# First chunk in halves of 256 tokens with six feature tiles ahead, two token tiles transposed by DMA, parameter arithmetic on GpSimd

## The chip, the cores and the metric

The kernel runs on one core of a Trainium2 chip. The metric is the device time of one execution in microseconds. Before the change it is 179.42 us, the median of 3 runs (179.28 to 179.64). The engines are named as in the profile: PE (TensorE matmul; PEld is its weight load), DVE (VectorE), ACT (ScalarE), POOL (GpSimd) and SP (SyncE, here only an issuer of DMAs). Each engine works off its own instructions in program order.

## What is computed

The input x is 2048 tokens of 512 features in bfloat16. It is normalised (layer norm without weights) to xn, and two layers of xn are added to x:

```python
xn = layernorm(x)
# A: a diagonal complex recurrence with 512 states
Lam_bar = exp(exp(log_dt) * (Lambda_re + 1j * Lambda_im))
B_bar   = ((Lam_bar - 1) / Lambda)[:, None] * (B_re + 1j * B_im)
Bu      = xn @ B_bar.T
h[t]    = Lam_bar * h[t - 1] + Bu[t]
A       = 2 * (h @ C.T).real + xn * Dskip
# B: a gated feed-forward layer with 1376 hidden features
Bf      = (silu(xn @ w_gate) * (xn @ w_up)) @ w_down
out     = x + A + Bf
```

## The kernel before, in words

**Tiling.** The 2048 tokens are four chunks of 512 (`NCH` = 4, `CW` = 512), each of four token tiles of 128 (`TPC` = 4). The hidden features are eleven feature tiles (`FT` = 11): ten of 128, and a last one of 96 whose columns are packed in their own tiles (`w_last`, `wu_last`). Every contraction over the 512 input features takes four matmuls (`KD` = 4) with the weights as the stationary operand and `xnT`, the normalised tokens transposed to features by tokens, as the moving one.

**Stages of one chunk.** `bproj_chunk` projects the chunk on the eight blocks of B (real and imaginary part, four blocks of states each; L357), ACT copies the results to SBUF (L359). `gateup_tile` makes gate and up of one feature tile (eight matmuls of 512 columns, L432), ACT evicts them from PSUM (Silu on L446, a cast on L447), DVE multiplies them in pairs (L451, queued in `products`). `ssm_ops` is the recurrence on DVE: a rotation by tables of cosine and sine (L367 to L381), eight scans (L399), a rotation back. `out_chunk` makes the output tiles on PE: `out_ffn` (L528) and `out_ssm` (L545).

**Order of the work.** The order of PE is written out. The work of DVE and part of ACT's lies in a `backlog`, a list of pieces with a cost each; `pump(us)` releases pieces as PE's work, in us, is written, `need(tag)` releases all that carry a tag, `multiply(keep)` releases products. For chunk 0 PE's order is: feature tiles 0 to 2 in pieces as the tokens come (`head_mm`, L631), tiles 3 to 6, the eight B projections, tiles 7 to 9, the last tile; then chunk 1 with `bproj_chunk(1)`.

**The head.** Nine dummy matmuls of 512 columns (L608) come first. For each of the four token tiles of chunk 0, DVE makes statistics (L185, L186), ACT makes 1/sqrt(var + eps) as Exp(-0.5 * Ln(var + eps)) (L190, L191), DVE normalises (L203), PE transposes in four blocks (L220), and ACT or DVE copies the two halves to `xnT` (L227, L229). The gate and up results of tiles 0 to 2 are kept in six of the eight PSUM banks until all 512 tokens are in. The 12 rows of parameters are transposed on PE as well (L250), cast by DVE (L253), and lead through `params_a`, `params_a2` and `params_sin` to the step `ws2` of the tables and the start values; between them ACT loads another function table (L259).

**Chunk 1's tokens.** `ln_rest(1, False)` gives its statistics (on DVE), a power on POOL (L195), four norms (L203, on DVE) and, after each, a DMA transpose on SP's queue (`xT_dma`, L234). They stand in the backlog with `table_ops`: for two of the four state blocks at a time a piece `turns` (L271), two pieces `half` (L277, L279, L280) on DVE, two sines on ACT (L284).

**Loads.** SP's queue issues x, the weights in the groups of `fgroups` (`load_w1`, L112), B transposed (L142), later the rest (`load_late`); ACT's queue issues three of the first ones; POOL's queue the parameters. DMAs from SP and ACT share eight semaphores in turn, so that each waits for the one eight places before it.

Of the kernel before, what the change touches and what calls it, by code (L numbers as in the profile page):

```python
# [23 lines left out]
def kernel(  # L24
# [17 lines left out]
    nc = tc.nc  # L42
# [30 lines left out]
    def bank(shape=(128, CW), dtype=F32):  # L73
        return psum.tile(list(shape), dtype, name="ps")
# [39 lines left out]

    neg_half = const.tile([128, TPC], F32, name="neg_half")
    nc.vector.memset(neg_half[:], -0.5)
    eps_t = const.tile([128, 1], F32, name="eps_t")
    nc.vector.memset(eps_t[:], EPS)

    nc.scalar.preload_act_table_set("natural_log_exp_and_others")  # L120

# [14 lines left out]
    for n in (TPC, TPC + 2):  # L136
        nc.sync.dma_start(out=xall[:, n:n + 2, :], in_=x_v[:, n:n + 2, :])
    load_w1(nc.sync, wg_g, wg_v, 2)
    load_w1(nc.sync, wu_g, wu_v, 2)
    for part, src in enumerate((A_B_re, A_B_im)):  # L140
        for k in range(KD):
            nc.sync.dma_start_transpose(out=BT[:, part, k, :], in_=src[:, k * 128:(k + 1) * 128])  # L142
        if part == 0:
            load_w1(nc.sync, wg_g, wg_v, 3)
            load_w1(nc.sync, wu_g, wu_v, 3)

    nc.sync.dma_start(out=w_last[:, :, 0:LB + LA], in_=wg_v[:, :, FL:F])
    nc.sync.dma_start(out=w_last[:, :, LB + LA:128], in_=wu_v[:, :, FL + LB:F])

    def load_late():  # L150
        nc.sync.dma_start(out=wu_last[:], in_=wu_v[:, :, FL:FL + LB])
# [29 lines left out]
    def xn_tile(c):  # L181
        return xn_end if c == NCH - 1 else xall[:, c * TPC:(c + 1) * TPC, :]
# [4 lines left out]

    def rstd_act(n):

        nc.scalar.activation(out=ve[:, n:n + 1], in_=mv[:, n, 1:2], func=ACT.Ln, bias=eps_t[:, 0:1])  # L190
# [10 lines left out]
    def norm_dve(n):  # L201
        c, i = divmod(n, TPC)
        nc.vector.tensor_scalar(out=xn_tile(c)[:, i, :], in0=xall[:, n, :], scalar1=mv[:, n, 0:1],  # L203
                                scalar2=rstd[:, n:n + 1], op0=ALU.subtract, op1=ALU.mult)

    def norm_act(n):
# [3 lines left out]

    HK = KD // 2

    def xT_pe(n, on_dve=(), prm_too=False):

        c, i = divmod(n, TPC)
        for h in range(2):
            tp = bank((128, HK * 128 + 128), BF16)
            for k in range(HK):
                lo = (h * HK + k) * 128
                nc.tensor.transpose(out=tp[:, k * 128:(k + 1) * 128], in_=xn_tile(c)[:, i, lo:lo + 128],  # L220
                                    identity=ident[:])
            if prm_too and h == 1:
                prm_transpose(tp[:, HK * 128:])
            dst = xnT[:, h * HK:(h + 1) * HK, n * 128:(n + 1) * 128]
            src = tp[:, 0:HK * 128].rearrange("p (k t) -> p k t", k=HK)
            if h in on_dve:
                nc.vector.tensor_copy(out=dst, in_=src)  # L227
            else:
                nc.scalar.copy(out=dst, in_=src)  # L229
        return tp[:, HK * 128:]  # L230

    def xT_dma(n):
        c, i = divmod(n, TPC)
# [12 lines left out]
    kk, fs1, fc1 = sm("kk", 2, NQ), sm("fs1", 2, NQ), sm("fc1", 2, NQ)  # L246
    V = nc.vector

    def prm_transpose(pp):
        nc.tensor.transpose(out=pp, in_=prm_rows[:], identity=ident[:])  # L250
# [44 lines left out]
    def tt(o, a, b, op):  # L295
        V.tensor_tensor(out=o, in0=a, in1=b, op=op)

    def params_sin():

        def turns(dst, shift):  # L300
            src = ws2[:]
            if shift:
                V.tensor_scalar(out=dst[:], in0=src, scalar1=shift, scalar2=None, op0=ALU.add)
                src = dst[:]
            V.tensor_scalar(out=kk[:], in0=src, scalar1=MAGIC, scalar2=MAGIC, op0=ALU.add, op1=ALU.subtract)
            tt(dst[:], src, kk[:], ALU.subtract)

        V.tensor_scalar(out=ws2[:, 1, :], in0=ws2[:, 0, :], scalar1=float(CW), scalar2=None, op0=ALU.mult)
        turns(fs1, 0.0)
        nc.scalar.activation(out=sin1[:], in_=fs1[:], func=ACT.Sin, scale=TWO_PI_LO)  # L310
        turns(fc1, 0.25)
        nc.scalar.activation(out=cos1[:], in_=fc1[:], func=ACT.Sin, scale=TWO_PI_LO)

    def params_b():
        tt(t_a[:], lre, lre, ALU.mult)
        tt(t_b[:], lim, lim, ALU.mult)
        tt(den[:], t_a[:], t_b[:], ALU.add)
        V.reciprocal(out=den[:], in_=den[:])
        tt(lbi[:], r_t[:], sin1[:, 0, :], ALU.mult)
        tt(lbr[:], r_t[:], cos1[:, 0, :], ALU.mult)  # L320
        V.tensor_scalar(out=lbr[:], in0=lbr[:], scalar1=-1.0, scalar2=None, op0=ALU.add)
        tt(t_a[:], lbr[:], lre, ALU.mult)
        tt(t_b[:], lbi[:], lim, ALU.mult)
        tt(num_re[:], t_a[:], t_b[:], ALU.add)
        tt(t_a[:], lbi[:], lre, ALU.mult)
        tt(t_b[:], lbr[:], lim, ALU.mult)
        tt(num_im[:], t_a[:], t_b[:], ALU.subtract)
        for dst, num, s in ((c2re, num_re, 2.0), (nc2re, num_re, -2.0), (nc2im, num_im, -2.0)):
            V.scalar_tensor_tensor(out=dst[:], in0=num[:], scalar=s, in1=den[:], op0=ALU.mult, op1=ALU.mult)

    def c_ops():

# [266 lines left out]

    GU = 8 * 0.2163  # L600
    BP = 4 * 0.2163
    H = 3
    held = [(bank(), bank()) for _ in range(H)]
    warm = held[0][0]

    def dummy(n, cols):
        for _ in range(n):
            nc.tensor.matmul(warm[:, 0:cols], lhsT=ones[:, 0:128], rhs=ones[:, 0:cols], start=True, stop=True)  # L608
# [15 lines left out]

    def head_mm(which, lo, hi, ks, fis):

        for fi in fis:
            for k in ks:  # L630
                nc.tensor.matmul(held[fi][which][:, lo * 128:hi * 128], lhsT=wslice((wg_g, wu_g)[which], fi, k),  # L631
                                 rhs=xnT[:, k, lo * 128:hi * 128], start=(k == 0), stop=(k == KD - 1))

    allk = range(KD)
# [12 lines left out]
    head_mm(0, 0, 1, range(0, HK), (0, 1))  # L647
    head_mm(0, 0, 1, range(HK, KD), (0, 1))
    xT_pe(1)
    rstd_act(2)  # L650
    head_mm(1, 0, 1, range(0, HK), (0, 1))
    head_mm(1, 0, 1, range(HK, KD), (0, 1))
# [4 lines left out]
    head_mm(0, 1, 2, range(0, HK), (0, 1))  # L657
    head_mm(1, 1, 2, range(0, HK), (0, 1))
    head_mm(0, 1, 2, range(HK, KD), (0, 1))
    head_mm(1, 1, 2, range(HK, KD), (0, 1))  # L660
    head_mm(0, 0, 2, allk, (2,))
    pp = xT_pe(2, on_dve=(0, 1), prm_too=True)
    head_mm(1, 0, 2, allk, (2,))
    norm_dve(3)
    params_a(pp)
    params_a2()
    head_mm(0, 2, 3, range(0, HK), range(H))
    head_mm(1, 2, 3, range(0, HK), range(H))
    xT_pe(3, on_dve=(0, 1))
    head_mm(0, 2, 3, range(HK, KD), range(H))  # L670
    head_mm(1, 2, 3, range(HK, KD), range(H))
# [7 lines left out]
    for fi in range(H):  # L679
        head_mm(0, 3, 4, allk, (fi,))  # L680
        head_mm(1, 3, 4, allk, (fi,))
        gu_out(0, fi, *held[fi])
        pump(GU / 4)
    pump(2.0)

    def bproj_chunk(c):
        need(f"ln{c}")
# [130 lines left out]
```

## Time and profile before

| what | value |
|---|---|
| median of 3 runs | 179.42 us |
| span of the profiled execution, first to last instruction | 177.3 us (its own time is not listed apart from the runs; the median lies 2.1 above the span) |
| mean granted PE clock by the record | 1.00 |
| PE transposes in the head | 16 of features, 1 of parameters |
| DMA transpose of a token tile: issue, to landing | 1.22 us, 2.4 us |
| Silu eviction and cast of 128x512 on ACT | 0.62 and 0.60 us |
| `params_b` on DVE, 16 operations on 128x4 | 31.99 to 34.02 us |

A row of a timeline gives the start from the beginning of the span, the length, the engine, the line of the kernel, the operation, what it writes and reads, the shape and how many instructions the row merges; in square brackets stands idle time before it and what ended that. The names are the program's: `ps` is a PSUM bank, `xall` the tokens, `pm` a scratch tile. "SPq" rows are the times in which SP's queue issues DMAs, not those in which data moves.

### The profile page before, as it was taken

The page shows a single profiled execution, that of the slowest core. Times are in us where ns is not written, and L with a number is a line of the kernel's source. Part 1 is how long each engine was busy: PE and PEld are TensorE (multiplying, and loading weights), DVE is VectorE, ACT ScalarE, POOL GpSimd, SP SyncE. Part 2 cuts the span into 40 slices and gives each one's busy share as a digit, 9 for nine tenths or more (in the row PEclk, how much of TensorE's full clock was granted, in tenths as well). Part 3 has the DMA queues.
Part 4 walks back from the last instruction along what each step waited for, and adds up shares of the span by engine and source line. Part 5 has one row for each costly group of instructions (what it writes and reads, how often), then busy time and mean ns, then how long its engine had stood idle before and what let it go on. Part 6 is the DMA issues. An engine that isn't in the chain of part 4 may idle for free.

```text
span 177.3 us, 2449 instructions
## 1 busy us (share of the span) xinstructions
PE 172.9 (97%) x900; PEld 83.6 (47%) x916; DVE 154.4 (87%) x238; ACT 94.7 (53%) x173; POOL 23.2 (13%) x29
## 2 busy tenths in 40 slices
PE   8999999999999999999999999999999999999993
PEld 2884444444444444444444444444444444444743
DVE  6789997999999977899999999999999999990033
ACT  4589696977499369914966662013766600220000
POOL 6003000001200140000700000014280000150000
DMA  5999749973041024900440000005469500072012
GB/s 163 316 264 239 148 90 261 334 126 89 0 96 26 0 52 96 355 0 0 60 62 2 0 0 4 0 0 61 58 97 177 86 0 0 0 85 33 4 50 69
DMA packets 29131, 15.53 MB, mean 88 GB/s; under 512 B 18848, under 2 KB 29056, under 8 KB 29088
## 3 DMA queue, kind: packets, MB, share of 16 engines
q1 hardware_dynamic: 24416, 11.41, 28.8%
q0 software_dynamic: 3456, 3.28, 13.7%
q10 hardware_dynamic: 1248, 0.69, 1.3%
q8 instruction: 7, 0.11, 0.3%
q14 instruction: 4, 0.03, 0.1%
HBM read 8.03 MB, written 5.24 MB: 75 GB/s over the span
## 4 chain that ended last, share of the span: by engine, by line
PE 98%; issue 1%; DVE 0%
PE ps L432 36%; PE ps L528 19%; PE ps L545 16%; PE ps L357 16%; PE ps L631 3%; PE ps L608 2%; PE ps L483 2%; PE ps L535 2%; PE ps L472 1%; PE ps L220 1%; DVE res L548 0%; PE ps L250 0%
## 5 line engine op out<-in xcount | busy, mean ns | idle before, releaser
L432 PE MATMUL ps<-xnT,wg 128*128 128x512 bf16 x144 | 37.8, 379 | 0.4
L432 PE MATMUL ps<-xnT,wu 128*128 128x512 bf16 x145 | 37.3, 379 | 0.0
L528 PE MATMUL ps<-wd_sb,guT 128*128 128x512 bf16 (+2 forms) x177 | 36.7, 355 | 0.2
L399 DVE TENSOR_TENSOR_SCAN g<-r_t,car,u 128x512 bf16<-128x512 f32 x24 | 28.8, 1264 | 0.0
L545 PE MATMUL ps<-CF,wt 128*128 128x512 bf16 (+2 forms) x141 | 28.2, 355 | 0.2
L357 PE MATMUL ps<-xnT,BT 128*128 128x512 bf16 x126 | 28.2, 379 | 0.1
L446 ACT ACTIVATE guT<-ps 128x512 bf16<-128x512 f32 x40 | 24.6, 615 | 5.0 <-PE ps L432 5.0
L447 ACT CAST u<-ps 128x512 bf16<-128x512 f32 x40 | 24.1, 602 | 5.2 <-PE ps L432 5.1
L528 PEld LDWEIGHTS <-guT 128*128 128x128 bf16 x180 | 16.9, 98 | 18.0
L432 PEld LDWEIGHTS <-wu 128*128 128x128 bf16 x148 | 14.5, 98 | 17.5
L432 PEld LDWEIGHTS <-wg 128*128 128x128 bf16 x148 | 14.4, 98 | 17.2
L555 ACT CAST res<-ps 128x512 bf16<-128x512 f32 x12 | 6.7, 594 | 28.1 <-PE ps L545 28.1
L556 POOL DMA_DIRECT2D out_dram<-res x12 | 10.5, 1041 | 78.0 <-ACT res L555 78.0
L545 PEld LDWEIGHTS <-wt 128*128 128x128 bf16 x144 | 13.4, 98 | 14.4 <-issue 0.4
L357 PEld LDWEIGHTS <-BT 128*128 128x128 bf16 x128 | 12.5, 98 | 15.1
L359 ACT CAST u<-ps 128x512 bf16<-128x512 f32 x32 | 17.6, 588 | 3.7 <-PE ps L357 3.6
L451 DVE TENSOR_TENSOR guT<-guT,u 128x1024 bf16<-128x1024 bf16 x20 | 13.5, 680 | 0.0
L548 DVE TENSOR_TENSOR res<-ps,xn_end 128x512 bf16<-128x512 f32 (+2 forms) x6 | 3.0, 514 | 11.8 <-PE ps L545 11.8
L195 POOL TENSOR_TENSOR rstd<-ve,neg_half 128x4 f32<-128x4 f32 x3 | 5.3, 1761 | 53.9 <-DVE ve L194 53.9
L367 DVE TENSOR_TENSOR pm<-u,c 128x2048 bf16<-128x2048 bf16 x8 | 9.8, 1221 | 1.2 <-ACT c L284 1.1
L185 DVE BATCH_NORM_STATS2 stats<-xall 128x6 f32<-128x512 bf16 x14 | 9.5, 676 | 0.4 <-DMA xall<-in_A_x_dram 0.4
L367 DVE TENSOR_TENSOR pm<-g,c 128x2048 bf16<-128x2048 bf16 x8 | 9.7, 1215 | 0.1
(108 smaller groups left out, 166.6 us busy)
## 6 DMA issues: line engine op xcount, KB each, us to landing
out_dram<-in_A_x_dram SPq DMA_DIRECT2D x1, 1536.0 KB, 7.0
out_dram<-res POOLq DMA_DIRECT2D x12, 128.0 KB, 3.0
out_dram<-xall POOLq DMA_DIRECT2D x3, 512.0 KB, 7.6
wd_sb<-in_B_w_down_dram SPq DMA_DIRECT2D x1, 1280.0 KB, 10.9
xall<-in_A_x_dram SPq DMA_DIRECT2D x1, 1024.0 KB, 6.1
xall<-in_A_x_dram SPq DMA_DIRECT2D x2, 256.0 KB, 4.6
wg<-in_B_w_gate_dram SPq DMA_DIRECT2D x1, 512.0 KB, 5.6
wu<-in_B_w_up_dram SPq DMA_DIRECT2D x1, 512.0 KB, 6.1
```

Source lines behind the costliest of these rows:

```text
L185: nc.vector.bn_stats(out=stats[:, n, :], in_=xall[:, n, :])
L357: nc.tensor.matmul(ps[:], lhsT=BT[:, part, k, q * 128:(q + 1) * 128], rhs=xnT[:, k, c * CW:(c + 1) * CW], start=(k == 0), stop=(k == KD - 1))
L359: nc.scalar.copy(out=u_tiles[c][:, part, q, :], in_=ps[:])
L367: V.tensor_tensor(out=t[:], in0=flat(src()[:, i]), in1=flat(tab[:]), op=ALU.mult)
L399: V.tensor_tensor_scan(out=g()[:, part, q, :], data0=r_t[:, q:q + 1].to_broadcast([128, CW]), data1=u_tiles[c][:, part, q, :], initial=ini ...
L432: nc.tensor.matmul(ps[:fs, lo:hi], lhsT=wslice(groups, fi, k), rhs=xnT[:, k, c * CW + lo:c * CW + hi], start=(k == 0), stop=(k == KD - 1))
L446: nc.scalar.activation(out=guT[:fs, fi, :], in_=psg[:fs], func=ACT.Silu)
L447: nc.scalar.copy(out=u_pair[c][:fs, fi % 2, :], in_=psu[:fs])
L451: products.append(lambda: V.tensor_tensor(out=g, in0=g, in1=u, op=ALU.mult))
L528: nc.tensor.matmul(o[:], lhsT=gu_tiles[c][:, fi, i * 128:(i + 1) * 128], rhs=wd_sb[:, fi, lo:hi], start=(fi == 0), stop=False)
L545: nc.tensor.matmul(o[:], lhsT=w_tiles[c][:, part, q, i * 128:(i + 1) * 128], rhs=CF[:, part, q, lo:hi], start=False, stop=(c > 0 and part ...
L556: nc.gpsimd.dma_start(out=out_v[:, n, :], in_=res[:], accum_op=ALU.add)
```

## The change

It has these parts:

- The weight groups are tiles 0-1, 2-3, 4-5 and 6-9. ACT's queue issues up of group 1 and both of group 2; SP's queue issues group 3, the tokens of chunk 1 (as one DMA) and B's transposes after the DMA transposes of token tiles 2 and 3 (`load_mid`). POOL's queue issues `w_last`, from the backlog behind chunk 1's statistics.
- Token tile 0 and 1 are normalised in two halves of 256 features; each half is transposed on PE and copied (first half DVE, second half ACT). Token tiles 2 and 3 are transposed by DMA.
- PE makes feature tiles 0 to 5 for the first 256 tokens, then for the second 256. A PSUM bank holds 256 tokens of two feature tiles; ACT evicts and DVE multiplies 512 columns at a time. Tiles 6 to 9 follow in full, and the eight B projections come after them (`G0` = 10), then the last tile.
- The sine tables stand further ahead in the backlog: five pieces ahead of chunk 1's statistics, two between these and the norms, three after.
- `params_b` runs on POOL but for its reciprocal; it multiplies by `den` in two operations of its own.
- `eps` is an immediate, not a tile.

The order of instructions that the changed program gives each engine: on ACT, Ln and Exp of token tile 1 stand behind the copy of token tile 0's second half; on DVE, the cast of the parameters stands behind the norm of token tile 3, and ahead of chunk 1's norms stand two `turns` pieces, three `half` pieces, six products of 512 columns, two of 1024 and the statistics. PE's first matmul of chunk 1's projection waits for the four DMA transposes of chunk 1.

```diff
-    fgroups = [(0, 2), (2, 3), (3, 7), (7, FT - 1)]
+    fgroups = [(0, 2), (2, 4), (4, 6), (6, FT - 1)]
...
-    load_w1(nc.sync, wu_g, wu_v, 1)
+    load_w1(nc.scalar, wu_g, wu_v, 1)
+    load_w1(nc.scalar, wg_g, wg_v, 2)
...
+    def load_mid():
+        load_w1(nc.sync, wg_g, wg_v, 3)
+        load_w1(nc.sync, wu_g, wu_v, 3)
+        nc.sync.dma_start(out=xall[:, TPC:2 * TPC, :], in_=x_v[:, TPC:2 * TPC, :])
+        for part, src in enumerate((A_B_re, A_B_im)):
+            for k in range(KD):
+                nc.sync.dma_start_transpose(out=BT[:, part, k, :], in_=src[:, k * 128:(k + 1) * 128])
+
+    def load_w_last():
+        nc.gpsimd.dma_start(out=w_last[:, :, 0:LB + LA], in_=wg_v[:, :, FL:F])
+        nc.gpsimd.dma_start(out=w_last[:, :, LB + LA:128], in_=wu_v[:, :, FL + LB:F])
...
-    def xT_pe(n, on_dve=(), prm_too=False):
+    def xT_pe(n, h, on_dve):
...
     def params_b():
-        tt(t_a[:], lre, lre, ALU.mult)
+        gt(t_a[:], lre, lre, ALU.mult)
...
         V.reciprocal(out=den[:], in_=den[:])
-        tt(lbi[:], r_t[:], sin1[:, 0, :], ALU.mult)
+        gt(lbi[:], r_t[:], sin1[:, 0, :], ALU.mult)
...
+        gt(num_re[:], num_re[:], den[:], ALU.mult)
+        gt(num_im[:], num_im[:], den[:], ALU.mult)
...
     dummy(9, CW)
     ln_stats(0)
     rstd_act(0)
+    load_w1(nc.scalar, wu_g, wu_v, 2)
     nc.vector.bn_stats(out=stats[:, 1, :], in_=xall[:, 1, :])
-    norm_dve(0)
+    norm_dve(0, 0, DH)
+    xT_pe(0, 0, True)
+    norm_dve(0, DH, D)
+    dummy(1, 128)
+    xT_pe(0, 1, False)
+    dummy(2, 128)
     nc.vector.bn_aggr(out=mv[:, 1, :], in_=stats[:, 1, :])
     rstd_act(1)
-    xT_pe(0, on_dve=(0,))
-    dummy(4, 128)
-    norm_dve(1)
+    head_mm(held, (0, 1), 0, 0, 1, kh[0])
+    head_mm(held, (0, 1), 0, 0, 1, kh[1])
+    norm_dve(1, 0, DH)
+    norm_dve(1, DH, D)
+    xT_pe(1, 0, True)
+    xT_pe(1, 1, False)
+    head_mm(held, (0, 1), 1, 0, 1)
     ln_stats(2)
     rstd_act(2)
     nc.vector.bn_stats(out=stats[:, 3, :], in_=xall[:, 3, :])
     norm_dve(2)
+    xT_dma(2)
     nc.vector.bn_aggr(out=mv[:, 3, :], in_=stats[:, 3, :])
     rstd_act(3)
     norm_dve(3)
+    xT_dma(3)
+    load_mid()
+    head_mm(held, (0, 1), 0, 1, 2, kh[0])
+    head_mm(held, (0, 1), 0, 1, 2, kh[1])
+    head_mm(held, (0, 1), 1, 1, 2)
+    pp = prm_transpose()
+    head_mm(held, (2, 3), 0, 0, 2)
     params_a(pp)
     params_a2()
     params_sin()
+    head_mm(held, (2, 3), 1, 0, 2)
+    head_mm(held, (4, 5), 0, 0, 2)
+    head_mm(held, (4, 5), 1, 0, 2)
     tables = table_ops()
     stats1, norm1 = ln_rest(1, False)
-    queue("ln1", stats1)
-    queue("tables", tables[:2])
+    queue("tables", tables[:5])
+    queue("ln1", stats1 + [(0.0, load_w_last)])
+    queue("tables", tables[5:7])
     queue("ln1", norm1)
-    queue("tables", tables[2:])
+    queue("tables", tables[7:])
...
+    more()
+    head_out(held, 0, 0)
+    head_mm(second, pairs[0], 0, 2, 3)
+    head_mm(second, pairs[0], 1, 2, 3)
+    pump(GU / 2)
...
-    G0 = 7
-    for fi in range(H, G0):
+    G0 = FT - 1
+    for fi in range(2 * NP, G0):
```

More of the change, by code (lines that the diff above doesn't have):

```diff
@@ L211 @@
     HK = KD // 2
-    def xT_pe(n, on_dve=(), prm_too=False):
+    def xT_pe(n, h, on_dve):
         c, i = divmod(n, TPC)
[L216 to L230, printed above, removed]
+        tp = bank((128, HK * 128), BF16)
+        for k in range(HK):
+            lo = (h * HK + k) * 128
+            nc.tensor.transpose(out=tp[:, k * 128:(k + 1) * 128], in_=xn_tile(c)[:, i, lo:lo + 128], identity=ident[:])
+        dst = xnT[:, h * HK:(h + 1) * HK, n * 128:(n + 1) * 128]
+        src = tp[:].rearrange("p (k t) -> p k t", k=HK)
+        if on_dve:
+            nc.vector.tensor_copy(out=dst, in_=src)
+        else:
+            nc.scalar.copy(out=dst, in_=src)
     def xT_dma(n):
@@ L247, with prm_transpose @@
     V = nc.vector
-    def prm_transpose(pp):
-        nc.tensor.transpose(out=pp, in_=prm_rows[:], identity=ident[:])
+    def prm_transpose():
+        pp = bank((128, 128), BF16)
+        nc.tensor.transpose(out=pp[:], in_=prm_rows[:], identity=ident[:])
+        return pp
     def params_a(pp):
@@ L623, in ln_rest, with head_mm, head_out @@
         return ops, tail
-    def head_mm(which, lo, hi, ks, fis):
+    def head_mm(sets, fis, which, lo, hi, ks=range(KD)):
+        base = lo * 128 // HALF * HALF
         for fi in fis:
+            p, j = place[fi]
             for k in ks:
-                nc.tensor.matmul(held[fi][which][:, lo * 128:hi * 128], lhsT=wslice((wg_g, wu_g)[which], fi, k),
+                nc.tensor.matmul(sets[p][which][:, j, lo * 128 - base:hi * 128 - base],
+                                 lhsT=wslice((wg_g, wu_g)[which], fi, k),
                                  rhs=xnT[:, k, lo * 128:hi * 128], start=(k == 0), stop=(k == KD - 1))
-    allk = range(KD)
+    def head_out(sets, p, half):
+        if half == 0:
+            head_u[p] = up_p.tile([128, 2, CW], BF16, name="u2")
+        cols = slice(half * HALF, (half + 1) * HALF)
+        a, b = pairs[p]
+        g, u = gu_tile(0)[:, a:b + 1:b - a, cols], head_u[p][:, :, cols]
+        nc.scalar.activation(out=g, in_=sets[p][0][:], func=ACT.Silu)
+        nc.scalar.copy(out=u, in_=sets[p][1][:])
+        products.append(lambda: V.tensor_tensor(out=g, in0=g, in1=u, op=ALU.mult))
+    pairs = ((0, 2), (1, 3), (4, 5))
+    place = {fi: (p, j) for p, fis in enumerate(pairs) for j, fi in enumerate(fis)}
+    head_u = {}
+    kh = (range(0, HK), range(HK, KD))
+    DH = D // 2
     dummy(9, CW)
@@ new lines @@
+    head_mm(second, pairs[0], 1, 2, 3)
+    pump(GU / 2)
+    more()
+    head_out(held, 1, 0)
+    head_mm(second, pairs[1], 0, 2, 3)
+    head_mm(second, pairs[1], 1, 2, 3)
+    pump(GU / 2)
+    multiply(1)
+    head_out(held, 2, 0)
+    for p in range(2):
+        head_mm(second, pairs[p], 0, 3, 4)
+        head_mm(second, pairs[p], 1, 3, 4)
+        head_out(second, p, 1)
+        pump(GU / 2)
+        multiply(1)
+    more()
+    head_mm(second, pairs[2], 0, 2, 4)
+    head_mm(second, pairs[2], 1, 2, 4)
@@ L686, in bproj_chunk @@
+    head_out(second, 2, 1)
+    pump(GU)
+    multiply(1)
     def bproj_chunk(c):
```

78 lines of the change are left out of this document (24 added, 54 removed).

## The prediction

> **What bounds the kernel now.** I read the page's busy times and the chain that ended last, then PE's timeline of the first 40 us, then the timelines of DVE and of SP's queue around the first chunk border. First the page:
>
> ```profile
> PE 172.9 (97%) x900; PEld 83.6 (47%) x916; DVE 154.4 (87%) x238; ACT 94.7 (53%) x173; POOL 23.2 (13%) x29
> ...
> PE 98%; issue 1%; DVE 0%
> ```
>
> PE works from 0.78 us to the end and the last chain is PE itself. So the time is PE's own work plus any wait the change puts before a matmul; work taken from or given to DVE, ACT or POOL counts only through such a wait. PE's timeline (start, length, instruction):
>
> ```profile
> 0.78 4.00 PE L608 MATMUL ps<-const-bfloat16-1.0 128*128 128x512 bf16 x9 [0.78 <-PEq L802]
> 4.76 0.61 PE L220 MATMUL ps<-ident,xall 128*128 128x128 bf16 x4
> ...
> 9.50 0.39 PE L220 MATMUL ps<-ident,xall 128*128 128x128 bf16 x4
> 9.72 0.50 PE L631 MATMUL ps<-xnT,wg 128*128 128x128 bf16 x6
> ...
> 11.73 1.03 PE L432 MATMUL ps<-xnT,wg 128*128 128x512 bf16 x3
> ...
> 31.59 7.07 PE L357 MATMUL ps<-xnT,BT 128*128 128x512 bf16 x31
> ```
>
> Two things to see. Four transposes cost PE 0.22 us (9.50 to 9.72), 56 ns each. And at 31.59 PE starts chunk 1's B projection, the first work that needs the tokens of chunk 1. DVE and SP's queue make those tokens:
>
> ```profile
> 13.60 0.66 DVE L185 BATCH_NORM_STATS2 stats<-xall 128x6 f32<-128x512 bf16 x1
> ...
> 14.59 0.88 DVE L271 TENSOR_SCALAR pm<-jidx,ws 128x512 f32<-128x512 f32 x2
> 15.50 0.69 DVE L279 TENSOR_SCALAR pm<-pm 128x1024 f32<-128x1024 f32 x1
> 16.23 1.22 DVE L280 SCALAR_TENSOR_TENSOR pm<-pm 128x1024 f32<-128x1024 f32 x1
> 17.37 0.69 DVE L451 TENSOR_TENSOR guT<-guT,u 128x1024 bf16<-128x1024 bf16 x1
> 17.97 1.38 DVE L203 TENSOR_SCALAR xall<-xall,mv,rstd 128x512 bf16<-128x512 bf16 x4
> ```
>
> ```profile
> 20.06 5.16 SPq L234 DMA_TRANSPOSE xnT<-xall  x4
> ```
>
> The four norms run at 17.97, the four DMA transposes issue from 20.06, 1.31 us apart, and land 2.4 to 2.5 us after issue: the last at 26.5, 5.1 us before PE needs it. That margin is what I check the change against.
>
> **The change, part by part** (times in us from the span's start; durations by the rows of before).
>
> *PE's work.* Eight transposes and one 128-column dummy go: 9 x 0.056 = -0.50. The matmul columns of feature tiles 0 to 5 in chunk 0 are equal (96 x 128 + 48 x 256 against 80 x 128 + 8 x 256 + 24 x 512), and 256 columns take 0.109, so smaller pieces cost nothing.
>
> *Token tile 0, in halves.* The first rstd is there at 4.29 in both. A half norm is not in the trace; between the 512-wide norm (0.41) and the 256-wide copy (0.29) I take 0.29. Then: norm half 4.29 to 4.58, transposes 4.64 to 5.03, DVE copy 5.07 to 5.36. The second half norm stands behind that copy on DVE: 5.28 to 5.57, transposes to 5.89, ACT copy 5.93 to 6.30. In before that copy started at 5.41: the second half is 0.5 later, the first 0.1 earlier.
>
> *Token tile 1.* Its Ln and Exp now stand behind that ACT copy; in before they stood ahead. Copy at 5.93, Ln at 6.20, Exp 6.52 to 6.73 (0.33 and 0.20 by their rows), half norms from 6.76 (before: 5.40), transposes 7.10 to 7.57, copies to 7.98. PE waits about 0.3 and then 0.5 here. Tiles 0 and 1 through feature tiles 0 and 1 are finished at 8.75; in before at 7.68. **+1.07**.
>
> *Feature tiles 2 to 5 for the first half:* 32 x 0.109, PE at 12.29 with the parameter transpose. Their weights are 1 MB behind the first 1 MB; in before 2.25 MB had landed at 10.3 (wg of 512 KB issued at 4.70, landing 5.6 later), so the last, wanted at 11.4, should be there by 10.5. Cost nothing; if that cover were gone, a few tenths.
>
> *Token tiles 2 and 3 by DMA.* DVE's copy, statistics and norms put tile 2's norm at 9.13 to 9.54 and tile 3's, behind ACT's Ln and Exp, at 10.23 to 10.64. Transposes issue at 9.58 and 10.88 and land 2.5 later: 12.1 and 13.4. PE wants them at 12.29 and 14.1. Hidden by 0.2 and 0.7.
>
> *PSUM.* The parameter cast now stands behind tile 3's norm on DVE: 10.55 (before 9.15). Through dt, dre and r_t (0.86), the table load (1.28) and two sines, ACT's first eviction comes at 12.9 (before 11.51), one each 0.48. Pair 1's second-half banks are pair 0's first-half ones: PE waits for them from 13.18 to 13.55 and a little at 14.0. **+0.39**. Six feature tiles are done at 18.0, before 16.92: +1.07 - 0.44 (transposes) + 0.39 and roundings, **+1.1**. All four remaining feature tiles (6.92) and chunk 0's B projection (6.92) and the last feature tile (0.87) follow, and PE is at chunk 1's projection at 32.7.
>
> *SP's queue* passes the moved loads: weights of tiles 6 to 9 at 12.2 and 12.8, x at 13.4, eight BT transposes 14.0 to 24.4. By 1.5 us per 512 KB these land at 15.4, 16.9, 18.4, BT's halves by 20.5 and 26; wanted at 18.0, 18.9, 21.1, 24.9 and 28.4. Hidden.
>
> *Chunk 1's norms, the term that decides.* In the new order DVE does before them: two turns, two "half" pieces of the sine tables, six products of 512, the statistics, two products of 1024, the other two turns and a third half. By start-to-start rows: turns 0.91 and 0.79; halves 1.87, 2.60, 1.85; statistics with ve 3.40; products 6 x 0.33 (half of 0.60 plus a little) and 2 x 0.60: 14.6 us of work, from 12.24 (end of the parameter chain), so 26.9 at the least. It also waits: 0.85 for the first evicted pair (ACT, 13.97), 0.65 for the fifth product (evicted 17.8), 0.25 for tile 9 (26.15). First norm at **28.6** (before 17.97). Then 0.41, four issues 1.31 apart, and 2.5 to land: 28.6 + 0.41 + 3 x 1.31 + 2.5 = 35.5, where PE stands since 32.7. **A wait of 2.8**, behind which all of PE's order stands.
>
> *GpSimd.* DVE loses 15 of 16 small operations (2.03 by 31.99 to 34.02), off the path. POOL gets 17. No such POOL row exists: bounds 0.10 (memset of one column) and 1.97 (the slowest pow on 128x4). I take 0.3, next to the 128x128 select (0.29), as pow is a long function. They have from 28 to 46.5, where POOL's next pow is due: nothing. The last feature tile's weights, now POOL's DMAs (0.5 to 1.04 each, landing within 4.6), land by 32.7 at the latest, wanted at 31.8; a delay would fall inside the 2.8.
>
> *After 35.5.* PE has the same 145.7 us left. DVE is about 3.0 behind its old place when chunk 0's rotation is done (the cosine table is late behind ACT's evictions), PE 3.9, so DVE is not worse off. SP's later transposes: C's issue ends at about 51.6 (before 42.9), chunk 2's tokens land near 59, wanted at 60.7. Nothing, with 1.5 to spare.
>
> **Sum:** 35.5 against 31.59, **+3.9**. The PE losses ahead of 32.7 are absorbed in it. The profiled span is 177.3; the runs' median 179.42 lies 2.1 above it, which I keep: 177.3 + 3.9 + 2.1 = **183.3**.
>
> **Clock.** The dummies of 512 columns stand 0.43 apart, later matmuls 0.216: PE is at half rate until about 5.35, though the clock column says 1.00. The new order leaves PE idle a few tenths before that point and 2.8 us at 32.7. *TensorE: Matmul & The Clock Gate* of the Trainium skill (What's actually happening) has the clock halved after an idle window of some 3.4 us and released after a busy one. By that rule 2.8 us is just not enough; if it were, a window at half rate would lose about 1.7 (an estimate from that page), 185.0. No row of before shows PE idle this long.
>
> **Rivals.**
> 1. *Chunk 1 is in time and only the head loses.* PE at 32.7: 177.3 + 1.1 + 2.1 = 180.5. It needs the norms at 25.8. Against: 14.6 us of DVE work after 12.24. For: I may have ACT's evictions and DVE's products too slow. 0.10.
> 2. *Faster: PE only loses work.* Half norms bring tile 1 no later and chunk 1 is ready: -0.5, 178.9. It decides if chunk 1's first norm starts by 24.2 (31.1 - 2.5 - 3.9 - 0.4). For: the eight transposes do go, and the tiles arrive by DMA in time. Against: Ln and Exp behind the ACT copy, and the same 14.6. 0.05.
> 3. *The idle PE falls back to half rate.* At the start half rate lasted 4.6 us, so up to 2.3 lost: 185.6. Decides if the wait grows past what the clock tolerates, which before can't show. 0.08.
> 4. *POOL's small operations are slow.* Over 1.1 us each, 17 of them pass 46.5, delay chunk 2's rstd and with it DVE, which waits in order for it: at 1.66, some 10 late, 187 and more. For: pow's 1.47 to 1.97 on the same shape. 0.05.
>
> **How the numbers follow.** Forecast 0.72, within 182.0 to 184.7 (a microsecond of DVE or ACT either way). The range takes in half of rival 3 and leaves out rivals 1, 2 and 4, 0.20: **181.2 to 185.4**. A measurement tells about 0.2% from no change. Faster 0.05; same 0.02 (between rivals 1 and 2); slower 0.93.
>
> **What would show it.** Chunk 1's first norm near 28.6 on DVE; SP's four transposes of xnT from 29 on; a PE gap of about 3 us before chunk 1's projection, released by the last of them; tile 1's norm near 6.8; a first eviction near 12.9. Wrong: norms before 26, no gap on PE, or a gap elsewhere (weights of tiles 2 to 5, PSUM, chunk 2's tokens).

## The result, and the profile after

The changed kernel takes 185.47 us in the median of four runs (183.23, 184.84, 186.10, 186.19), the kernel before beside it on the same chip 179.35 us (179.18 to 179.64). It is **slower**: the ratio is 1.026 (95% interval 1.023 to 1.029). This ratio is taken from the two faster runs of the changed kernel, 184.04 us on average, because the other two lie more than 1.5% above its fastest. Forecast were 183.3 us, 181.2 to 185.4: the two faster runs lie inside that range, 186.10 and 186.19 above it.

Three of the four runs show a mean PE clock of 0.99, and only the fastest shows 1.00. The profiled execution (span 184.4 us) is the slowest of the four. Its page:

```profile
PE 177.0 (96%) x939; PEld 87.3 (47%) x939; DVE 153.3 (83%) x224; ACT 97.1 (53%) x172; POOL 35.5 (19%) x48
...
PEclk9999999969999999999999999999999999999999
...
PE 93%; ACT 3%; DVE 1%; DMA 1%; issue 0%
```

PE is busy for 4.1 us more although 0.5 us of its work was taken away; one slice of the clock row, the ninth (36.9 to 41.5 us), reads 6 where all others read 9; and the last chain is no longer PE alone. PE's timeline (start, length, instruction, idle before it):

```profile
5.89 0.39 PE L217 MATMUL ps<-ident,xall 128*128 128x128 bf16 x2 [0.53 <-DVE xall L201]
...
8.77 1.06 PE L636 MATMUL ps<-xnT,wg 128*128 128x128 bf16 x8
9.62 0.76 PE L636 MATMUL ps<-xnT,wu 128*128 128x128 bf16 x8
...
13.76 0.61 PE L636 MATMUL ps<-xnT,wg 128*128 128x128 bf16 x8
...
32.90 1.03 PE L485 MATMUL ps<-xnT,w_last 128*128 128x512 bf16 x4
36.94 8.75 PE L359 MATMUL ps<-xnT,BT 128*128 128x512 bf16 x32 [3.02 <-ACT c L279]
```

Three things are to be seen. Eight matmuls of 128 columns take 1.06 us at 8.77 and 0.61 at 13.76: PE is at half rate until about 9.85 us, where in the kernel before it was until 5.35. Then PE stands idle for 3.02 us before chunk 1's B projection. And the 32 matmuls of that projection take 8.75 us, in the kernel before 7.07. What PE waits for, on DVE and SP's queue:

```profile
29.86 1.40 DVE L201 TENSOR_SCALAR xall<-xall,mv,rstd 128x512 bf16<-128x512 bf16 x4
```

```profile
30.32 5.16 SPq L227 DMA_TRANSPOSE xnT<-xall  x4
```

Chunk 1's norms begin at 29.86 (before: 17.97) and the transposes issue from 30.32. By the trace's DMA records they land at 32.74, 34.07, 35.37 and 36.70; PE starts at 36.94. The row names ACT's cosine table as releaser, because that instruction ended at 36.79, after the last landing. Which of the two counts is the first question to the chip.

The stretch around the resumption (start:end and length, busy time and instruction count of PE, PEld, DVE, ACT and POOL, the granted clock, DMA share, GB/s):

```profile
34.00:37.00 3.00, 0.06 (x1) 0.09 (x2) 0.18 (x1) 2.75 (x4) 0.25 (x2) 1.00 0.46 92
37.00:41.00 4.00, 4.00 (x12) 1.45 (x12) 3.97 (x5) 1.17 (x2) 1.65 (x3) 0.57 0.94 254
41.00:45.00 4.00, 4.00 (x20) 1.84 (x19) 3.90 (x6) 2.48 (x5) 3.26 (x3) 1.00 1.08 358
```

With the clock at 0.57 PE gets 12 matmuls done in 4 us, afterwards 20.

**Where the 7.1 us of the profiled execution went.** Chunk 1's projection starts at 36.94 instead of 31.59: 5.35, of which 3.02 is the wait and 2.33 the head. From chunk 1's projection to chunk 2's it is 26.72 us (36.94 to 63.66), before 25.03 (31.59 to 56.62): 1.69 lost to the clock. From chunk 2's to chunk 3's it is 43.40 in both. Together 7.04. The other runs fit the same parts: in 183.23 the clock stayed at 1.00; 184.84 lies 1.61 above it, one fall of the clock; 186.10 and 186.19 lie another 1.3 above. I put that last step down to the head's half rate ending early or late. The traces of experiments 1 and 3, whose head is that of the changed kernel, show both cases, 1.2 us apart; the unprofiled runs cannot show which case they are.

### The profile page after: what moved, and what is told of

Read it like the earlier page. It is cut to its first block, busy times and chain, and to the rows that moved or that the text cites. A ratio compares the mean times of both kernels' runs of the same rounds, so it can differ in the third digit from the quotient of the medians.

```text
span 184.4 us, 2520 instructions
## 1 busy us (share of the span) xinstructions
PE 177.0 (96%) x939; PEld 87.3 (47%) x939; DVE 153.3 (83%) x224; ACT 97.1 (53%) x172; POOL 35.5 (19%) x48
## 3 DMA queue, kind: packets, MB, share of 16 engines
q0 software_dynamic: 3536, 3.41, 13.9%
## 4 chain that ended last, share of the span: by engine, by line
PE 93%; ACT 3%; DVE 1%; DMA 1%; issue 0%
PE ps L434 32%; PE ps L530 19%; PE ps L359 16%; PE ps L547 15%; PE ps L636 6%; PE ps L537 2%; PE ps L485 1%; DMA xall<-in_A_x_dram 1%; PE ps L474 1%; PE ps L217 1%; ACT c L279 1%; DVE xall L201 1%; ACT s L279 1%; DVE stats L183 0%; ACT u L361 0%
## 5 line engine op out<-in xcount | busy, mean ns | idle before, releaser
L530 PE MATMUL ps<-wd_sb,guT 128*128 128x512 bf16 (+2 forms) x180 | 36.9, 355 | 0.0
L434 PE MATMUL ps<-xnT,wu 128*128 128x512 bf16 x136 | 34.9, 379 | 0.0
L434 PE MATMUL ps<-xnT,wg 128*128 128x512 bf16 x136 | 34.9, 379 | 0.0
L359 PE MATMUL ps<-xnT,BT 128*128 128x512 bf16 x128 | 30.0, 395 | 3.0 <-ACT c L279 3.0
L530 PEld LDWEIGHTS <-guT 128*128 128x128 bf16 x180 | 16.9, 98 | 18.0
L361 ACT CAST u<-ps 128x512 bf16<-128x512 f32 x32 | 18.8, 586 | 11.2 <-PE ps L359 11.2
L448 ACT ACTIVATE guT<-ps 128x512 bf16<-128x512 f32 x34 | 20.3, 598 | 6.3 <-PE ps L434 6.2
L449 ACT CAST u<-ps 128x512 bf16<-128x512 f32 x34 | 20.0, 589 | 6.4 <-PE ps L434 6.4
L359 PEld LDWEIGHTS <-BT 128*128 128x128 bf16 x128 | 12.9, 101 | 19.6 <-issue 5.7
L434 PEld LDWEIGHTS <-wu 128*128 128x128 bf16 x136 | 13.3, 98 | 16.0
L434 PEld LDWEIGHTS <-wg 128*128 128x128 bf16 x136 | 13.3, 98 | 15.8
L547 PEld LDWEIGHTS <-wt 128*128 128x128 bf16 x144 | 13.4, 98 | 14.4 <-issue 0.4
L453 DVE TENSOR_TENSOR guT<-guT,u 128x1024 bf16<-128x1024 bf16 x17 | 11.5, 678 | 1.1 <-ACT u L449 1.1
```

Source lines behind the costliest of these rows:

```text
L359: nc.tensor.matmul(ps[:], lhsT=BT[:, part, k, q * 128:(q + 1) * 128], rhs=xnT[:, k, c * CW:(c + 1) * CW], start=(k == 0), stop=(k == KD - 1))
L361: nc.scalar.copy(out=u_tiles[c][:, part, q, :], in_=ps[:])
L434: nc.tensor.matmul(ps[:fs, lo:hi], lhsT=wslice(groups, fi, k), rhs=xnT[:, k, c * CW + lo:c * CW + hi], start=(k == 0), stop=(k == KD - 1))
L448: nc.scalar.activation(out=guT[:fs, fi, :], in_=psg[:fs], func=ACT.Silu)
L449: nc.scalar.copy(out=u_pair[c][:fs, fi % 2, :], in_=psu[:fs])
L453: products.append(lambda: V.tensor_tensor(out=g, in0=g, in1=u, op=ALU.mult))
```

## The experiments

Times are medians; the kernel before ran beside each at 179.2 us in the median (single runs 179.0 to 179.7). Theory A: chunk 1's late norms, through the four DMA transposes, set the wait, and the fall of the clock follows from the wait's length. Rival B: ACT's cosine table sets it. Rival C: the head's order is what costs.

**1. The norms ahead of the next table pieces.**

```diff
     queue("ln1", stats1 + [(0.0, load_w_last)])
-    queue("tables", tables[5:7])
     queue("ln1", norm1)
-    queue("tables", tables[7:])
+    queue("tables", tables[5:])
```

> Only the backlog's order differs from the changed kernel: the four norms of chunk 1 stand right behind its statistics, ahead of the second pair of turns and its first half piece (2.7 us of DVE work). Theory A, the norms set the wait: in the changed kernel's profile the norms start at 29.86, SP's four transposes at 30.32, the last lands at 36.70 and PE resumes at 36.95. Here the norms wait only for POOL's power, start near 26.6, the last transpose lands near 33.5, before PE gets there (33.8): no wait, no fall of the clock, 180.0 to 181.3 us. Rival B, PE waits for ACT's cosine table (the profile names ACT c L279, which ends at 36.79 in that profile, as what ended the wait): the same DVE pieces still come before the table, it ends near 36.8 again, PE resumes near 36.9 and the time stays at 183 to 186 us.

Measured: 181.8 us (181.12 to 182.52), ratio 1.0145 (1.0108 to 1.0181). DVE, SP's queue and PE in its trace:

```profile
26.24 0.44 DVE L201 TENSOR_SCALAR xall<-xall,mv,rstd 128x512 bf16<-128x512 bf16 x1 [1.16 <-POOL rstd L193]
```

```profile
26.71 5.89 SPq L227 DMA_TRANSPOSE xnT<-xall  x4
```

```profile
34.06 7.07 PE L359 MATMUL ps<-xnT,BT 128*128 128x512 bf16 x32 [0.23 <-DMA xnT<-xall]
```

The norms come 3.6 us earlier and the wait shrinks from 3.02 to 0.23 us. ACT's cosine table stands where it stood (in the changed kernel at 35.73):

```profile
35.64 1.06 ACT L279 ACTIVATE c<-pm 128x1024 bf16<-128x1024 f32 x1
```

It ends at 36.70, and PE started 2.6 us before that. The projection runs at full rate (7.07). A holds, B falls: the profile names what ended last, and that was a coincidence. PE would have been at the projection at 33.83 without the wait, in the kernel before at 31.59, so 2.2 us are left to the head.

**2. Token tile 1's Ln and Exp ahead of the copy, as in the kernel before.**

```diff
     norm_dve(0, 0, DH)
+    nc.vector.bn_aggr(out=mv[:, 1, :], in_=stats[:, 1, :])
+    rstd_act(1)
     xT_pe(0, 0, True)
...
-    nc.vector.bn_aggr(out=mv[:, 1, :], in_=stats[:, 1, :])
-    rstd_act(1)
```

> Only the place of token tile 1's aggregate, Ln and Exp differs from the changed kernel: ahead of token tile 0's transposes, as in the kernel before. Theory A: tile 1's norm starts near 5.6 in place of 7.07, the first eviction near 12.2 in place of 13.22, chunk 1's norms about 1.3 earlier (28.5), the last transpose lands near 35.3; the wait stays at 2.5 to 3 us, so 182 to 185 us (the upper end where the clock falls in the wait). Rival C, the loss is in the head and the later wait only its echo: with the head mended the wait closes as well and the time is 180 us or less.

Measured: 184.31 us (184.07 to 184.43), ratio 1.0283 (1.0267 to 1.0298), PE clock 0.99 in every run. In its trace PE is at the second 256 tokens at 11.71 instead of 13.76 (the head's half rate also ended earlier in this execution: from 4.8 us on matmuls of 128 columns stand 0.055 apart). Of these two microseconds 1.2 are won in the median, and nothing against the two faster runs of the changed kernel (184.04):

```profile
31.12 1.03 PE L485 MATMUL ps<-xnT,w_last 128*128 128x512 bf16 x4
35.02 8.56 PE L359 MATMUL ps<-xnT,BT 128*128 128x512 bf16 x32 [2.88 <-ACT c L279]
```

PE comes to the projection earlier and waits there as before. The norms moved with the head (27.96), so 1.9 us are won at 35.02, but the wait and the fall of the clock stay. C falls as the main cause. How much of the 2.05 us is the order and how much the half rate can be read from the next trace.

**3. Work in the wait.** Twelve dummy matmuls of 512 columns ahead of chunk 1's projection, into a bank that nobody reads.

```diff
         need(f"ln{c}")
+        if c == 1:
+            fill = bank()
+            for _ in range(12):
+                nc.tensor.matmul(fill[:], lhsT=ones[:, 0:128], rhs=ones[:], start=True, stop=True)
```

> The changed kernel with twelve dummy matmuls of 512 columns (2.6 us at full rate) into an unused bank ahead of chunk 1's projection, so that PE works while it waits. Theory A with the clock falling because PE idles: PE still resumes near 36.9 in a profile like the changed kernel's, but its first matmuls there stand 0.216 apart and not 0.43; every run shows a mean clock of 0.998 or more, the median falls by about 1.8 to between 183 and 184.5 us. Rival D, the clock falls for another reason (the load of that moment, chance): the clock stays at 0.99 in most runs, 185 to 186 us.

Measured: 184.13 us (183.17 to 184.87), ratio 1.0288 (1.0264 to 1.0312); three of four runs at a clock of 1.00, one at 0.99. I had expected all four. The trace of one:

```profile
32.56 2.78 PE L740 MATMUL ps<-const-bfloat16-1.0 128*128 128x512 bf16 x12
35.62 7.07 PE L359 MATMUL ps<-xnT,BT 128*128 128x512 bf16 x31 [0.27 <-ACT c L279]
```

The gap is filled, not removed, yet the projection runs in 7.07 us instead of 8.75. The spread of the head hides the size; the next one removes that.

Up to the dummies this trace is the changed kernel's own order, and here the half rate of the head ended at about 3.6 us instead of 9.85:

```profile
12.44 0.61 PE L636 MATMUL ps<-xnT,wg 128*128 128x128 bf16 x8
```

```profile
28.54 1.38 DVE L201 TENSOR_SCALAR xall<-xall,mv,rstd 128x512 bf16<-128x512 bf16 x4
```

PE is 1.32 us earlier at the second 256 tokens than in the changed kernel's trace (13.76), and DVE 1.32 earlier at chunk 1's norms (29.86). In experiment 1's trace, where the half rate lasted to about 9.6, PE is there at 13.67. So the end of the half rate is worth 1.2 to 1.3 us with the same instructions, and of the 2.05 us of experiment 2 the order has 0.73 (11.71 against 12.44).

**4. Edits 2 and 3 together.**

> The kernel of e2_rstd_ahead (which showed a mean clock of 0.988 to 0.991 in all four runs) with the twelve dummy matmuls of 512 columns ahead of chunk 1's projection. If the clock falls because PE idles there: 0.998 or more in all runs, PE resumes at the same place (near 35.0) at full rate, 182.2 to 182.9 us, 1.5 to 1.9 below e2. If it falls for another reason: 184.0 to 184.5 as in e2.

Measured: 182.56 us (182.48 to 182.75), ratio 1.019 (1.0177 to 1.0204), clock 1.00 in every run. Against edit 2 alone this is 1.75 us less, for twelve matmuls **added**. PE resumes where it did in experiment 2 (35.02), now at full rate:

```profile
35.05 7.07 PE L359 MATMUL ps<-xnT,BT 128*128 128x512 bf16 x32 [0.26 <-ACT c L279]
```

PE's idleness, not the lateness of the tokens, is what the clock answers to.

**5. More dummies in the head.**

```diff
-    dummy(1, 128)
+    dummy(8, 128)
     xT_pe(0, 1, False)
```

> The changed kernel with eight in place of one dummy matmul of 128 columns between the transposes of token tile 0's two halves, where PE idles 0.5 to 0.8 us. If that gap is what keeps PE at half rate (matmuls of 128 columns 0.107 apart up to 9.8 in the changed kernel's profile, up to 5.3 in the one before): they stand 0.056 apart from about 5.4 on, the second half starts near 12.5 in place of 13.76. By theory A little of it reaches the end, as the norms of chunk 1 move only where DVE waited for an eviction: 0.5 to 1.3 us less, 182 to 185 us. If the gap isn't the reason: half rate up to 9.8 again and no gain.

Measured: 185.92 us in the median of three runs (184.87 to 186.42), ratio 1.0364 (1.0324 to 1.0404): no gain, a miss. A fourth execution, the profiled one, took 309.79 us at a clock of 0.56 from end to end; it is left out, and I have no cause for it. So no trace here shows the edit's head at the usual clock, and whether the head's half rate hangs on the short gaps there stays open.

**6. The late order alone, in the kernel before.**

```diff
-    queue("ln1", stats1)
-    queue("tables", tables[:2])
-    queue("ln1", norm1)
-    queue("tables", tables[2:])
+    queue("tables", tables[:5])
+    queue("ln1", stats1)
+    queue("tables", tables[5:7])
+    queue("ln1", norm1)
+    queue("tables", tables[7:])
```

> The kernel before with one part of the change alone: its backlog in the order five table pieces, statistics of chunk 1, two table pieces, norms of chunk 1, the rest. By the rows of the profile before, DVE's norms of chunk 1 move from 17.97 to 24.4 or 25, the last DMA transpose lands at 31.3 to 32 in place of 26.5, and PE wants it at 31.59. Theory A (this order eats the margin of 5.1 us, and the later parameter chain, the products and the later B projection in the changed kernel turn it into a wait): 179.2 to 179.9 us, with a wait of 0 to 0.5 us ahead of chunk 1's projection. Rival: the order alone makes the whole wait of 3 us: 182 us.

Measured: 179.75 us (179.61 to 180.13), ratio 1.0035 (1.0022 to 1.0048). The norms slide from 17.97 to 24.55 and the 5.1 us of margin are used up:

```profile
24.55 1.38 DVE L203 TENSOR_SCALAR xall<-xall,mv,rstd 128x512 bf16<-128x512 bf16 x4
```

```profile
32.15 7.07 PE L357 MATMUL ps<-xnT,BT 128*128 128x512 bf16 x32 [0.37 <-ACT u L447]
```

By the trace's DMA records the last transpose landed at 32.01, just ahead of PE. The order alone thus costs about 0.6 us; it becomes a wait of 3 us only together with the rest of the change, which starts everything ahead of the norms later (x of chunk 1 behind the weights, the first eviction at 13.22, six small products). Which of these counts most was not tested.

**7. A mended version.** Whole norms and the earlier kernel's order in token tiles 0 and 1, the parameter cast ahead of tile 3's norm, the tokens of chunk 1 loaded ahead of the weights of tiles 6 to 9, and the backlog `tables[:2]`, statistics, `tables[2:3]`, norms, `tables[3:]`.

> The changed kernel with whole norms and the order of before in token tiles 0 and 1 (Ln and Exp of tile 1 ahead of tile 0's transposes), the parameter cast ahead of tile 3's norm, chunk 1's tokens loaded ahead of the last weight group, and chunk 1's statistics and norms behind two and three table pieces. Halves of 256 tokens, the DMA transposes of token tiles 2 and 3, and GpSimd's arithmetic stay. Theory A: no wait ahead of chunk 1's projection and none in tile 1, so PE only loses eight transposes (0.44) and may wait 0.3 for PSUM: 178.7 to 179.5 us, against 179.2 before. Rival: something else in the new head (weights of tiles 2 to 5, DMA transposes, PSUM) costs as well: 180 us or more.

Measured: 181.24 us (181.07 to 181.67), ratio 1.0119 (1.0106 to 1.0132): a miss. Chunk 1's projection no longer waits, but the exchange of the loads was my own mistake:

```profile
17.27 1.04 PE L434 MATMUL ps<-xnT,wg 128*128 128x512 bf16 x4 [0.29 <-DMA wg<-in_B_w_gate_dram]
18.94 1.04 PE L434 MATMUL ps<-xnT,wu 128*128 128x512 bf16 x4 [0.63 <-ACT guT L448]
```

Weights for tiles 6 to 9 arrive late: by the DMA records they land at 17.23 and 18.89, just before PE resumes (the second row again names an instruction that only ended last). A further 0.60 us is lost at chunk 2's projection.

**8. The same with token tiles 2 and 3 transposed on PE.**

> The kernel of e7_mended with token tiles 2 and 3 transposed by PE and copied by DVE as in the kernel before; SP's queue then issues the later loads at once. Eight transposes of 0.056 come back to PE: 0.3 to 0.6 us above e7_mended, if the DMA transposes are hidden there. Below e7_mended, if they are not.

Measured: 184.84 us (184.6 to 186.47), ratio 1.0348 (1.0313 to 1.0383). It was to price the transposes and does not, since another thing moved:

```profile
10.41 1.05 PE L636 MATMUL ps<-xnT,wu 128*128 128x256 bf16 x8 [0.35 <-DMA wu<-in_B_w_up_dram]
...
12.82 1.05 PE L636 MATMUL ps<-xnT,wg 128*128 128x256 bf16 x8 [1.14 <-DMA wg<-in_B_w_gate_dram]
...
14.94 1.05 PE L636 MATMUL ps<-xnT,wu 128*128 128x256 bf16 x8 [1.07 <-DMA wu<-in_B_w_up_dram]
```

Without the two DMA transposes at its head, SP's queue issues the next tokens at 2.67 and the last weight group at 3.26 and 5.52, and they compete with the weights that PE needs first. In the changed kernel the transposes, which wait for the norms, also hold those loads back.

**9. Mended again.** As 7, but with the loads in the order of the change, the backlog of experiment 1, and chunk 2's statistics two scans earlier.

```diff
-    queue("ssm0", fwd0[0:2] + [(1.5, params_b)] + fwd0[2:6])
+    queue("ssm0", fwd0[0:2] + [(1.5, params_b)] + fwd0[2:4])
     stats3, norm3 = ln_rest(3, True)
     queue("ln2", stats2)
-    queue("ssm0", fwd0[6:8])
+    queue("ssm0", fwd0[4:8])
```

> The mended head (whole norms, the order of the kernel before in token tiles 0 and 1) with the loads in the order of the change (weights of the third group, then the second chunk's tokens), chunk 1's statistics and norms queued together behind the first five table operations, and chunk 2's statistics two scans earlier. Theory (the costs found so far, the late norms and the dearer head, are all that the change costs, and the waits for weights and for chunk 2's tokens came from the first mending's own load order): 179.2, range 178.9 to 179.8, ratio 0.997 to 1.002; six feature tiles' head ends near 16.8, weights of the next tiles come without a wait, chunk 1's projection begins at 31.5 to 31.9. Rival (the tokens of chunk 1 come too late behind the weights for six tiles ahead, whatever the order): a wait of 0.8 or more at chunk 1's projection, 180.3 or more.

Measured: 180.10 us (180.00 to 180.28, five runs, clock 1.00), ratio 1.0044 (1.0031 to 1.0057), 0.3 above the range I gave; the rival's 0.8 us of wait is not there either.

```profile
30.61 1.03 PE L485 MATMUL ps<-xnT,w_last 128*128 128x512 bf16 x4
32.12 7.07 PE L359 MATMUL ps<-xnT,BT 128*128 128x512 bf16 x32 [0.48 <-DMA xnT<-xall]
```

The head ends at 16.80 and the next weights come without a wait. Of the change's loss (4.7 us in its two faster runs, 6.1 in the median of four) all but 0.9 is undone by order and whole norms (up to 1.3 of it may be the head's half rate, which ended by 5.1 us in this trace), with the halves by 256 tokens, the DMA transposes and GpSimd's arithmetic kept. What is left at this point is 0.53 us (32.12 against 31.59), nearly all of it the wait of 0.48 for chunk 1's tokens: the last transpose lands at 31.87. The chunk's x, at 18.58, is not what holds this up: its statistics begin only at 19.40.

**10. The parameter arithmetic back on VectorE**, in the kernel of 9.

> The second mended kernel with the small parameter operations back on VectorE: that part of the change alone. Theory (forecast: hidden on GpSimd, and nothing waits for them on VectorE either): the same as the second mended kernel within 0.3 us. Rival (GpSimd's slower operations hold up the rotation): 0.5 to 1.5 faster. Other rival (VectorE's 16 operations of about 0.07 to 0.16, some 1.5 us, push chunk 2's norms past their due time): 0.5 to 1.5 slower, with a wait at chunk 2's projection.

Measured: 182.66 us (182.42 to 183.93), ratio 1.0198 (1.0173 to 1.0224), so 2.6 us slower than 9 (180.10). The second rival, that VectorE's operations push chunk 2's norms, is seen:

```profile
33.40 7.07 PE L352 MATMUL ps<-xnT,BT 128*128 128x512 bf16 x32 [1.40 <-DMA xnT<-xall]
...
59.44 2.75 PE L352 MATMUL ps<-xnT,BT 128*128 128x512 bf16 x12 [0.84 <-DMA xnT<-xall]
```

The 16 operations occupy DVE from 37.17 to 39.20; in 9 only the reciprocal stands there, and chunk 2's tokens were in time. I can put the 0.84 us at 59.44 down to this. The other 0.9 us of wait, at 33.40, come from ahead of the edit: in this trace the half rate of the head lasted to about 6.7 us, in 9 PE was at full rate by 5.1, and DVE is 0.73 later at its first norms of chunk 1 (24.77 against 24.04). Why all runs of 9 lie together and all but one run of 10 lie 2.3 to 2.7 above them is open.

**11. The eight transposes on PE, with the DMA transposes still running** into a tile that nobody reads, in the kernel of 9.

> The second mended kernel with token tiles 2 and 3 transposed on TensorE again, while the two DMA transposes still run (into a tile that nobody reads), so that the sync queue and the loads behind it keep their times: the TensorE part of that edit alone. Theory (the eight transposes cost their TensorE time): 0.4 to 0.6 slower than the second mended kernel; with the VectorE copies they need, at most 1.2 slower. Rival (the time is given back by a later wait): within 0.2.

Measured: 181.69 us (181.56 to 182.18), ratio 1.0136 (1.0119 to 1.0153), 1.6 slower than 9: more than the PE time and more than the 1.2 I allowed. PE is at feature tile 6 at 17.38 instead of 16.80. The longer half rate is in that too, but it ends before the parameter transpose (8.07 here, 7.93 in 9), and from there to tile 6 PE takes 9.31 us instead of 8.87: 0.44 more, eight transposes of 0.056. The rest shows as waits behind SP's queue, the longest

```profile
30.00 2.98 PE L364 MATMUL ps<-xnT,BT 128*128 128x512 bf16 x13 [1.03 <-DMA BT<-in_A_B_im_dram]
```

whose loads were issued some 2 us later than in 9 (20.93 against 18.86). So the direct price fits, and the total is not settled.

## Why the prediction was right, and where it was not

**The deciding term was right.** First norm 28.6 forecast, 29.86 measured; last transpose landed 35.5, measured 36.70; wait 2.8, measured 3.02. Experiment 1 shows that this chain, and not the table that the profile names, sets the start. The place and size of the mechanism were right; the 1.2 us by which all of it is later come from the half rate in the head. In experiment 3's trace, where that ended early, the forecast's steps stand almost where they were put: tile 1's norm at 6.76 (6.76 forecast), PE free at 32.56 (32.7), first norm at 28.54 (28.6), last transpose landed at 35.37 (35.5). The one run in which the mean clock stayed up, 183.23, lies at the forecast of 183.3; it has no trace, so its parts are not shown. That the ratio's two runs lie inside the range is in part luck: the late end of the half rate (1.2 to 1.3) and the fall of the clock (1.5 to 1.7) were in no term of the sum, and two of four runs lie above the range by 0.7 to 0.8.

**The head's clock was left out.** "+1.07" and "+1.1" were forecast for the head. In the profiled execution PE would have reached the projection at 33.92 instead of 31.59, so +2.33. The order of the steps was right: tile 1's norm stands behind ACT's copy, at 7.07 (6.76 forecast). The forecast saw that PE would idle there before the half rate ends, and put no term on it. What I missed is that the matmuls there run at half rate until 9.85, so that eight of 128 columns cost 0.86 instead of 0.45: second 256 tokens at 13.76, forecast 12.29. The gap on DVE in front of tile 1's norm:

```profile
7.07 0.60 DVE L201 TENSOR_SCALAR xall<-xall,mv,rstd 128x256 bf16<-128x256 bf16 x2 [1.14 <-ACT rstd L189]
```

Experiment 2 removes it; this order is worth 0.73 us and the clock 1.32 (experiment 3). With the half rate ended early the last feature tile starts at 31.70 against 30.73 before, so the head then costs 0.97, near the 1.1 forecast. Because the wait absorbs the head, the error did not reach the sum directly; it came back through DVE, which starts chunk 1's chain that much later.

**PSUM: less than forecast.** The first eviction was to be at 12.9 and is at 13.22, but PE was later still, so the "+0.39" does not show. In experiment 2, where PE is early, it is there as 0.3 (at 12.85). **The half norm** is 0.34 alone and 0.60 for two, forecast 0.29 each.

**The clock: the rival that happened.** "By that rule 2.8 us is just not enough" was the weakest sentence. The row decides: after 3.02 us idle in the profiled run and 2.88 in experiment 2, the granted clock fell to 0.57 and 0.61 over the next 4 us, and the loss was 1.69 and 1.50 us (chunk 1's projection to chunk 2's, against 25.03 before). By the mean clock of each run it fell in three of four runs of the changed kernel, in experiment 2 in all four; with dummies in the gap in none of four (experiment 4) and one of four (experiment 3). The mean does not say where: one of four runs of experiment 1 shows 0.991 as well, and that kernel's trace has no such wait. The forecast gave this 0.08. *TensorE: Matmul & The Clock Gate* of the Trainium skill (What's actually happening) asks for an idle window of some 3.4 us; its table for kernel writers (Why this matters for your kernels) says no gaps over about 3 us. The second number is the one these traces come near; the first they contradict by 0.4 to 0.5 us.

**GpSimd: hidden, as forecast, though slower.** The operations take 0.19 to 1.29 us each where I took 0.3. The twelve that need no reciprocal are done by 34.33 in the changed kernel, the rest between 39.35 and 44.26, and POOL's next power starts at 47.67 after waiting 3.41 us for DVE, so nothing hung on them. My rival 4 put the limit at 1.1 us for all of them; the mean is 0.64 (10.96 us over 17). *GPSIMD Engine Reference* of the Trainium skill (3.1) keeps to VectorE for elementwise work. On durations the trace agrees (0.13 to 0.18 us on DVE for the same shape); for the time of this kernel it is the other way, since DVE's order is what PE waits for and GpSimd's is not (0.84 us in experiment 10).

**Hidden loads: right.** Weights of tiles 2 to 5 landed by 10.1 (forecast 10.5), token tiles 2 and 3 at 12.46 and 13.84 (12.1 and 13.4), SP's weights at 17.25 and 18.70 (15.4 and 16.9), all before PE came, and so also in experiment 3's trace, where PE is earlier (token tile 2 lands at 12.04, PE starts on it at 12.44). Experiment 7 shows how thin it is: weights 1.5 to 1.8 us later than in experiment 9 (15.69 and 17.13) cost 0.9 us.

**Behind the projection: right, with less to spare.** From chunk 2 on both kernels take the same 43.40 us to chunk 3. But the 1.5 us to spare for chunk 2's tokens holds only because PE is late: in experiments 1, 7 and 10, where PE is earlier, it waits 0.2, 0.6 and 0.84 there.

**PE's own work, -0.5:** the transposes are gone, and experiment 11 finds their price (0.44), yet nothing of it reached the end; even the second mended kernel is 0.44% (0.31 to 0.57) slower than the kernel before.

## What to carry to other kernels

When a kernel's busiest engine never waits, look at the margin of each border between stages before reordering what feeds it: here 5.1 us on four DMA transposes were spent by putting table work, small products and a later start ahead of them. Price such a wait with the clock in mind: if it nears 3 us, count the slow matmuls after it too, and if it can't be removed, cheap matmuls in the gap are worth more than they cost. A queue whose first entry waits also holds back all that follows, for worse or (experiment 8) for better, so removing the entry is never a test of the entry alone.

## What the runs showed of the hardware

- An idle PE of 2.9 to 3.0 us by the rows was followed by a stretch at half rate: matmuls of 512 columns 0.43 apart from 37.2 to 40.6 in the changed kernel, beginning about 0.2 us after PE resumed, and from the resumption at 35.02 to 38.0 in experiment 2. One of four runs of the changed kernel got by without, by its mean clock.
- The clock records of these two traces put the half rate at 37.22 to 40.64 and 34.67 to 38.09, 3.41 us each, and the full rate before it at 27.31 and 30.72 us, which is 8 and 9 times as long; the full stretches of seven other traces (170.67 to 177.49) are whole multiples of it too. So the clock appears to change only at ticks 3.41 us apart, which lie differently in each execution. That would let equal waits end differently, and the head's half rate too; no run here tests it.
- The half rate at the start ended anywhere between about 3.6 and 9.85 us in these traces; with the same instructions (changed kernel and experiment 3) that was worth 1.3 us. I could not steer it (experiment 5).
- Operations of 128x4 on POOL vary from 0.19 to 1.29 us for the same instruction; the long ones fall at other places in other kernels (`nc2re` 1.28 in the changed kernel, 0.21 in experiment 9).
- One execution ran slowly from end to end: 309.79 us at a clock of 0.56. No cause is known.
